# Gate and up products of two row blocks in one pass over the weight tiles, and two attention numerators moved to a later pass

## The chip, the cores and the metric

The kernel runs on one NeuronCore of a Trainium2 chip. The metric is the device time of one execution in microseconds, lower is better. Times of one kernel scatter by some tenths of a microsecond from run to run.

The profile's names: PE is TensorE's row of matmuls, PEld its row of weight loads, DVE is VectorE, ACT is ScalarE, POOL is GpSimd. SBUF is the on-chip memory that holds inputs and weights; PSUM is where matmuls write, used here as eight banks of 512 columns. L361 is line 361 of the kernel.

## The reference

A gated mix of two branches over the same x of 2048 x 640 (bf16). What matters here:

```python
a = attention(x)                                   # linear attention, 32 heads of 20
b = (gelu(x @ w_gate) * (x @ w_up)) @ w_down       # 640 -> 1728 -> 640
g = sigmoid((x * gate_w).sum(-1, keepdims=True))
return g * a + (1 - g) * b
```

The attention ends, for each tile of 128 rows, in a numerator and a denominator (`num = phi_q @ kv`, `den = phi_q @ z`) and their quotient.

## The kernel before

x lies transposed in SBUF (`xT`), in four blocks of 512 columns (rows of x). The 1728 inner features are cut in 13 chunks of 128 and one of 64. For a full chunk, gate is five matmuls (contraction 640 = 5 x 128) into one PSUM bank, and up is five into another. For the last one ("chunk 13"), gate and up share one set of five matmuls and one bank. ScalarE then makes gelu of the gate bank, and VectorE multiplies it by the up bank:

```python
def gateup(self, b, c, banks):
    ...
    slot = self.gn % 3
    self.gn += 1
    if c < 13:
        for w, wk, bk in ((self.wg_sb, "wg", banks[0]), (self.wu_sb, "wu", banks[1])):
            for kt in range(self.KD):                # KD = 5
                self.mm(bk, 0, 512, w[:, kt, c * P:(c + 1) * P], xs(kt), kt == 0, kt == self.KD - 1, ...)
        sc.op("act", lambda e: e.activation(self.gl[:, slot, :], self.bank(banks[0]), AF.Gelu_apprx_tanh), ...)
        sc.op("dve", lambda e: e.tensor_tensor(hT, self.bank(banks[1]), self.gl[:, slot, :], ALU.mult), ...)
    else:
        ...   # chunk 13: five matmuls, one gelu of 64 rows, two half products of 64 rows
```

`self.mm` issues a matmul that always brings its own weight load. The chunks run in the order 0, 1, 13, 2, ..., 12. I call their position in that order the *place*, so chunk 13 stands at place 2. Full chunks alternate between the bank pairs (0,1) and (6,7): a pair is wanted again two places later.

The numerator of a tile is twenty small matmuls into banks 2 to 5, then a chain of eleven VectorE instructions (reciprocals, products with 32 columns, two products and a sum with 640 columns), and at its end a transposing DMA into `goT`:

```python
def num(self, t):
    for i in range(self.KD):
        for s in (0, 1):
            for r in (0, 1):
                ... matmul of 64 rows x 88 columns into bank NUMB + 2 * r + s ...
    ... eleven VectorE instructions, one after the other ...
```

```python
def first_nums(idx):
    if idx in (4, 8):                        # after places 4 and 8
        self.num(idx // 4 - 1)
...
gateups(0, state)
gateups(1, first_nums)
gateups(2, none)
gateups(3, none)
for b in range(self.NB):
    downs(b, ...)                            # w_down and wo, with the other 14 numerators
```

The timelines show VectorE's instructions in the order in which the program issues them.

The softmax here doesn't subtract the row's maximum and nothing guards it: scores larger than these inputs give would overflow.

Of the kernel before, what the change touches and what calls it, by code (L numbers as in the profile page):

```python
# [3 lines left out]
P = 128  # L4
BF16 = mybir.dt.bfloat16
F32 = mybir.dt.float32
AF = mybir.ActivationFunctionType
ALU = mybir.AluOpType
# [99 lines left out]
class _Kernel:  # L108
# [528 lines left out]
            return self.xT[:, c // 3, (c % 3) * self.BT:(c % 3 + 1) * self.BT]  # L637
        return (self.hT0, self.hT1, self.hT2)[b][:, c, :]

    def gateup(self, b, c, banks):  # L640
        sc = self.sc
        xs = lambda kt: self.xT[:, kt, b * self.BT:(b + 1) * self.BT]
        xr = [("xT", t) for t in range(4 * b, 4 * b + 4)]
        old = (self.oldw, self.oldk, [], [("xT", t) for t in range(12)])[b]
        hT, hk = self.hT(b, c), b
        slot = self.gn % 3
        self.gn += 1
        if c < 13:
            i = 0 if c < 7 else 1
            for w, wk, bk in ((self.wg_sb, "wg", banks[0]), (self.wu_sb, "wu", banks[1])):  # L650
                for kt in range(self.KD):
                    self.mm(bk, 0, 512, w[:, kt, c * P:(c + 1) * P], xs(kt), kt == 0, kt == self.KD - 1, xr + [(wk, i)])
            sc.op("act", lambda e: e.activation(self.gl[:, slot, :], self.bank(banks[0]), AF.Gelu_apprx_tanh),  # L653
                  reads=[("ps", banks[0])], writes=[("gl", slot)], guard=self.oldw)
            sc.op("dve", lambda e: e.tensor_tensor(hT, self.bank(banks[1]), self.gl[:, slot, :], ALU.mult),  # L655
                  reads=[("ps", banks[1]), ("gl", slot)], writes=[("hT", hk, c)], guard=old)
        else:
            bk = banks[0]
            for kt in range(self.KD):
                self.mm(bk, 0, 512, self.wgu_sb[:, kt, :], xs(kt), kt == 0, kt == self.KD - 1, xr + ["wgu0", "wgu1"])  # L660
            sc.op("act", lambda e: e.activation(self.gl[64:128, slot, :], self.ps[0:64, bk * 512:bk * 512 + 512],
                                                AF.Gelu_apprx_tanh),
                  reads=[("ps", bk)], writes=[("gl", slot)], guard=self.oldw)
            for r in (0, 1):
                odd = lambda v: v.rearrange("p (u r q) -> p u r q", r=2, q=P)[:, :, r, :]
                sc.op("dve", lambda e: e.tensor_tensor(
                    odd(hT[64 * r:64 * r + 64, :]), odd(self.ps[64:128, bk * 512:bk * 512 + 512]),
                    odd(self.gl[64:128, slot, :]), ALU.mult),
                    reads=[("ps", bk), ("gl", slot)], writes=[("hT", hk, c, r)], guard=old)

    def num(self, t):
        sc = self.sc
# [113 lines left out]
    def ffn(self):  # L786
        self.gn = 0
        self.pn = 0
        pairs = [(0, 1), (6, 7)]

        def gateups(b, after):
            for idx, c in enumerate([0, 1, 13] + list(range(2, 13))):
                self.gateup(b, c, pairs[self.pn % 2])
                self.pn += 1
                after(idx)

        def downs(b, side):
            p = [pairs[(self.pn + k) % 2] for k in (0, 1)]
            n = 0
            for t in (4 * b, 4 * b + 2):  # L800
                final = t + 2 == self.NT
                for _ in self.down_pair(t, p + [(2, 3)] if final else p, (256, 256, 128) if final else (320, 320)):
                    n += 1
                    if n in side:
                        self.num(side[n])

        def state(idx):
            if idx < 3:
                self.gram(13 + idx)
            if idx == 2:  # L810
                self.columns = False
                self.kv_evac()
                self.gates()
                self.kv_ones()
            if 6 <= idx < 11:
                self.kv_mask(idx - 6)

        def first_nums(idx):
            if idx in (4, 8):
                self.num(idx // 4 - 1)  # L820

        def none(idx):
            pass
        at = (1, 31, 61, 91)
        gateups(0, state)
        gateups(1, first_nums)
        gateups(2, none)
        gateups(3, none)
        for b in range(self.NB):
            downs(b, {at[k]: 4 * b + 2 + k for k in range(4 if b < 3 else 2)})  # L830

# [43 lines left out]
```

## Time and profile before

| | before |
|---|---|
| time, median | 286.4 us (286.36 to 286.82) |
| span of the profiled run | 285.0 us |
| matmuls (PE), busy | 281.1 us (99%) |
| weight loads (PEld), busy | 186.1 us (65%) |
| VectorE busy / ScalarE busy | 174.4 / 105.2 us |

The first part of the page: each engine, its busy time, the share of the span and the number of instructions.

```profile
PE 281.1 (99%) x3045; PEld 186.1 (65%) x3060; DVE 174.4 (61%) x352; ACT 105.2 (37%) x200; POOL 5.3 (2%) x36
```

The chain that ended last, by engine and by line, is all TensorE:

```profile
PE 99%; issue 0%; ACT 0%
PE ps L361 62%; PE ps L737 28%; PE ps L681 2%; PE ps L373 2%; PE ps L468 2%; PE ps L341 1%; PE ps L557 1%; PE ps L298 0%; ACT outsb L750 0%; PE ps L564 0%; PE ps L323 0%
```

PE busy at 99% alone does not say that nothing is to be had: matmuls are pipelined, and their records (379 ns each) overlap. What counts is the distance from one matmul to the next. It can be read from VectorE's timeline in the pass of block 1, where nothing but PE paces it. The columns are start, duration, what ran, and in brackets the idle time before it and what ended it.

```profile
103.85 0.69 DVE L655 TENSOR_TENSOR hT<-ps,gl 128x512 bf16<-128x512 f32 x1 [0.72 <-PE ps L361]
106.01 0.69 DVE L655 TENSOR_TENSOR hT<-ps,gl 128x512 bf16<-128x512 f32 x1 [1.47 <-PE ps L361]
108.17 0.69 DVE L655 TENSOR_TENSOR hT<-ps,gl 128x512 bf16<-128x512 f32 x1 [1.47 <-PE ps L361]
110.32 0.69 DVE L655 TENSOR_TENSOR hT<-ps,gl 128x512 bf16<-128x512 f32 x1 [1.47 <-PE ps L361]
112.48 0.69 DVE L655 TENSOR_TENSOR hT<-ps,gl 128x512 bf16<-128x512 f32 x1 [1.47 <-PE ps L361]
```

One product per chunk; four chunks of ten matmuls take 112.48 - 103.85 = 8.63 us, so 215.8 ns a matmul of 512 columns. The Trainium skill (TensorE: Matmul & The Clock Gate, "Wait — 56ns, not 53.3ns?") gives N/2.4 + about 2.5 ns for back-to-back matmuls, 215.7 ns for N = 512. The trace agrees, and it does so with a weight load in front of every matmul. The groups of these loads, from the list that keeps shapes apart:

```profile
L361 PEld LDWEIGHTS ps<-xT,wu_sb 128*128 128x128 bf16 x250 | 24.5, 98 | 29.5
L361 PEld LDWEIGHTS ps<-xT,wg_sb 128*128 128x128 bf16 x250 | 24.2, 98 | 29.0 <-ACT gl L653 0.2
```

A load takes 98 ns (the second number after the bar). It runs beside the matmul in front of it, and in this stage the load row is idle more than half the time.

The first numerator, in block 1 of the kernel before, first PE's timeline and then VectorE's:

```profile
116.81 1.03 PE L361 MATMUL ps<-xT,wu_sb 128*128 128x512 bf16 x4
117.77 0.57 PE L681 MATMUL ps<-KV,Eq 64*128 64x88 bf16 x20
118.27 1.25 PE L361 MATMUL ps<-xT,wg_sb 128*128 128x512 bf16 x5
...
122.60 1.24 PE L361 MATMUL ps<-xT,wg_sb 128*128 128x512 bf16 x5
123.89 1.03 PE L361 MATMUL ps<-xT,wu_sb 128*128 128x512 bf16 x4
```

```profile
117.88 0.69 DVE L655 TENSOR_TENSOR hT<-ps,gl 128x512 bf16<-128x512 f32 x1 [1.47 <-PE ps L361]
118.59 0.36 DVE L697 RECIPROCAL RH<-ps 128x32 f32<-128x32 f32 x1
...
122.31 0.49 DVE L710 TENSOR_TENSOR Og<-O,O 128x640 bf16<-128x640 bf16 x1
122.72 1.28 DVE L655 TENSOR_TENSOR hT<-ps,gl 128x512 bf16<-128x512 f32 x2
```

The chain holds VectorE from 118.59 to 122.72, 4.13 us. The product of the chunk after the numerator (place 5) waits behind it and ends at 122.72 + 0.69 = 123.41. PE wants that chunk's up bank again for place 7, right after the gate matmuls that began at 122.60, that is at 122.60 + 5 x 0.2158 = 123.68. (The up group at 123.89 shows four matmuls: the record of its first, at 123.67, is missing.) So the numerator fits with 0.27 us to spare.

### The profile page before, as it was taken

To read this page: it belongs to the slowest core of one execution; us is meant where nothing else is said; L and a number is where in the kernel's file an instruction comes from. 1 tells how busy PE (TensorE), PEld (TensorE's weight loads), DVE (VectorE), ACT (ScalarE), POOL (GpSimd) and SP (SyncE) were. 2 spreads that over 40 slices of the span, in tenths; PEclk is the share of its full clock that TensorE was granted. 3 is DMA by queue.
4 is the path that set the end of the run, shared out by engine and by line. 5 is a ranking of instruction groups with operands and counts; after the bars stand their busy time and mean duration, and the time that the engine had idled before them with its cause. 6 is when DMAs were issued, how large, how long until landed. Compare 5 with 4: busy or idle time off the path is not lost.

```text
span 285.0 us, 7066 instructions
## 1 busy us (share of the span) xinstructions
PE 281.1 (99%) x3045; PEld 186.1 (65%) x3060; DVE 174.4 (61%) x352; ACT 105.2 (37%) x200; POOL 5.3 (2%) x36
## 2 busy tenths in 40 slices
PE   8999999999999999999999999999999999999996
PEld 4665799999984444444444444445777777777786
DVE  1459999999976652667242334225883883883801
ACT  4367898667754223222322223221112112112021
POOL 7000000000000000000000000000000000000000
DMA  8999993000002000011000000000233223322421
GB/s 228 225 199 313 361 349 111 2 0 2 2 0 48 0 0 2 2 23 25 0 0 0 2 0 0 0 2 0 26 82 58 50 62 59 70 52 68 71 72 48
DMA packets 36937, 18.67 MB, mean 66 GB/s; under 512 B 28970, under 2 KB 36394, under 8 KB 36906
## 3 DMA queue, kind: packets, MB, share of 16 engines
q1 hardware_dynamic: 36240, 18.19, 26.3%
q8 instruction: 24, 0.39, 0.6%
q10 hardware_dynamic: 666, 0.03, 0.2%
q14 instruction: 7, 0.06, 0.1%
HBM read 9.04 MB, written 2.62 MB: 41 GB/s over the span
## 4 chain that ended last, share of the span: by engine, by line
PE 99%; issue 0%; ACT 0%
PE ps L361 62%; PE ps L737 28%; PE ps L681 2%; PE ps L373 2%; PE ps L468 2%; PE ps L341 1%; PE ps L557 1%; PE ps L298 0%; ACT outsb L750 0%; PE ps L564 0%; PE ps L323 0%
## 5 line engine op out<-in xcount | busy, mean ns | idle before, releaser
L361 PE MATMUL ps<-xT,wg_sb 128*128 128x512 bf16 (+1 forms) x265 | 63.8, 379 | 0.4 <-issue 0.2
L361 PE MATMUL ps<-xT,wu_sb 128*128 128x512 bf16 (+1 forms) x263 | 63.3, 379 | 0.4
L653 ACT ACTIVATE gl<-ps 128x512 bf16<-128x512 f32 x52 | 30.9, 596 | 72.9 <-PE ps L361 70.7
L655 DVE TENSOR_TENSOR hT<-ps,gl 128x512 bf16<-128x512 f32 x39 | 26.6, 689 | 38.8 <-PE ps L361 38.7
L737 PE MATMUL ps<-wd_sb,hT 64*128 64x320 bf16 x648 | 48.5, 296 | 0.0
L361 PEld LDWEIGHTS ps<-xT,wu_sb 128*128 128x128 bf16 (+1 forms) x270 | 26.6, 99 | 29.5
L361 PEld LDWEIGHTS ps<-xT,wg_sb 128*128 128x128 bf16 (+1 forms) x270 | 26.2, 99 | 29.0 <-ACT gl L653 0.2
L361 PE MATMUL ps<-w,xT 128*64 128x512 bf16 (+6 forms) x398 | 41.5, 325 | 0.1
L750 ACT ACTIVATE outsb<-ps,Gm 128x320 bf16<-128x320 f32 (+2 forms) x31 | 14.5, 515 | 72.4 <-PE ps L737 72.4
L737 PEld LDWEIGHTS ps<-wd_sb,hT 64*128 64x128 bf16 x648 | 31.1, 94 | 12.2 <-issue 0.4
L361 PEld LDWEIGHTS ps<-w,xT 128*64 128x64 bf16 (+1 forms) x400 | 35.9, 107 | 4.5
L737 PE MATMUL ps<-wo_sb,goT 64*128 64x320 bf16 (+2 forms) x340 | 26.5, 288 | 0.0
L361 PE MATMUL ps<-xT,wq 128*64 128x512 bf16 (+1 forms) x184 | 26.0, 380 | 0.1
L438 DVE TENSOR_REDUCE Dk<-Ek 128x64 f32<-128x1280 bf16 x16 | 23.7, 1478 | 3.7 <-ACT gcol L426 3.7
L452 DVE TENSOR_TENSOR Ek<-Ek,Dk 128x640 bf16<-128x640 bf16 x32 | 25.0, 821 | 0.6
L708 DVE TENSOR_TENSOR O<-ps,RH 128x640 bf16<-128x640 f32 x32 | 24.7, 815 | 0.0
L423 ACT ACTIVATE Ek<-ps 128x640 bf16<-128x640 f32 x32 | 20.7, 703 | 4.2 <-PE ps L361 4.2
L537 ACT ACTIVATE Eq<-ps 128x512 bf16<-128x512 f32 x40 | 21.6, 607 | 0.6 <-PE ps L361 0.4
L655 DVE TENSOR_TENSOR xT<-ps,gl 128x512 bf16<-128x512 f32 x13 | 9.0, 690 | 18.2 <-PE ps L361 18.2
L737 PEld LDWEIGHTS ps<-wo_sb,goT 64*128 64x128 bf16 x340 | 16.0, 94 | 5.3
L361 PEld LDWEIGHTS ps<-xT,wq 128*64 128x64 bf16 (+1 forms) x185 | 15.4, 108 | 2.9
L737 PE MATMUL ps<-wd_sb,xT 64*128 64x320 bf16 (+2 forms) x270 | 16.0, 269 | 0.0
(71 smaller groups left out, 173.8 us busy)
## 6 DMA issues: line engine op xcount, KB each, us to landing
out_dram<-outsb SPq DMA_DIRECT2D x7, 320.0 KB, 2.3
wd_sb<-in_B_w_down_dram SPq DMA_DIRECT2D x1, 2080.0 KB, 12.9
wg_sb<-in_B_w_gate_dram SPq DMA_DIRECT2D x1, 1120.0 KB, 7.4
wu_sb<-in_B_w_up_dram SPq DMA_DIRECT2D x1, 1120.0 KB, 9.8
wg_sb<-in_B_w_gate_dram SPq DMA_DIRECT2D x1, 960.0 KB, 9.1
wu_sb<-in_B_w_up_dram SPq DMA_DIRECT2D x1, 960.0 KB, 9.3
w<-in_A_wqkv_dram SPq DMA_DIRECT2D x5, 160.0 KB, 3.6
wo_sb<-in_A_wo_dram SPq DMA_DIRECT2D x1, 800.0 KB, 8.5
```

The lines of the kernel that those rows point to most:

```text
L361: self.sc.op("pe", lambda e: e.matmul(self.ps[a:z, bank * 512 + c0:bank * 512 + c0 + n], lhs[:, a:z], rhs, start=first, stop=fin), reads=r ...
L373: sc.op("pe", lambda e, c0=c0, n=n, bk=bk, col=col: e.matmul(self.bank(bk)[:, col:col + n], self.xT[:, kt, t * P:(t + 1) * P], self.w3[:, ...
L423: self.sc.op("act", lambda e, s=s, scale=scale: e.activation(self.Ek[:, se, s, :], self.ps[:, o:o + self.D], AF.Exp, scale=scale), reads=[ ...
L438: sc.op("dve", lambda e: e.tensor_reduce(self.Dk[:, se, 0, :].rearrange("p (s h) -> p s h", h=H), self.Ek[:, se, :, :].rearrange("p s (h d ...
L452: sc.op("dve", lambda e, v=v, r=r: e.tensor_tensor(v, v, r, ALU.mult), reads=[("Rk", se)], writes=[("Ek", se, s)])
L468: sc.op("pe", lambda e: e.matmul(self.ps[a:a + 64, b * 512 + c:b * 512 + c + 2 * nf], va[:, lo:lo + 64], self.Ek[:, se, :, f0:f0 + nf], st ...
L537: sc.op("act", lambda e, s=s, scale=scale: e.activation(self.Eq[:, s, i, b * self.BT:(b + 1) * self.BT], self.bank(bank), AF.Exp, scale=sc ...
L653: sc.op("act", lambda e: e.activation(self.gl[:, slot, :], self.bank(banks[0]), AF.Gelu_apprx_tanh), reads=[("ps", banks[0])], writes=[("g ...
L655: sc.op("dve", lambda e: e.tensor_tensor(hT, self.bank(banks[1]), self.gl[:, slot, :], ALU.mult), reads=[("ps", banks[1]), ("gl", slot)], ...
L708: dve(lambda e, o=o, f=f, s=s: e.tensor_tensor(o, V[s][:, :, :, 0:DH], f, ALU.mult), rb + [key(6 + s)], [("O", s, sl)], guard=old)
L737: sc.op("pe", lambda e: e.matmul(self.bank(bk, w), lhs, rhs, start=opens and x == 0, stop=end and not opens, skip_group_check=True), reads ...
L750: sc.op("act", lambda e: e.activation(dst, self.bank(bk, w), AF.Copy, scale=g), reads=rd, writes=wr)
```

## The change

The intent: take blocks 1 and 2 in one pass, so that each tile of w_gate and w_up is loaded once and used by two matmuls, one for each block. The second of a pair is issued without a weight load. The joint pass needs four banks for a chunk and four for the next, all eight, so no numerator fits into it; the first two numerators move to block 3's pass.

```diff
+    def mm_again(self, bank, n, lhs, rhs, first, fin, reads):
+        ...   # InstMatmult(..., ldweights=False): uses the weights that are in the array
-    def gateup(self, b, c, banks):
+    def gateup(self, bs, c, gate, up):
...
+        def mms(w, keys, banks):
+            for kt in range(self.KD):
+                for k, b in enumerate(bs):
+                    a = (512, w(kt), xs(b, kt), kt == 0, kt == self.KD - 1, xr(b) + keys)
+                    if k:
+                        self.mm_again(banks[k], *a)
+                    else:
+                        self.mm(banks[k], 0, *a)
...           # gelu and product as before, once for each block of bs
         def first_nums(idx):
-            if idx in (4, 8):
-                self.num(idx // 4 - 1)
+            if idx in (2, 6):
+                self.num((idx - 2) // 4)
...
-        gateups(0, state)
-        gateups(1, first_nums)
-        gateups(2, none)
-        gateups(3, none)
+        gateups((0,), state)
+        gateups((1, 2), none)
+        gateups((3,), first_nums)
```

More of the change, by code (lines that the diff above doesn't have):

```diff
@@ L638, in hT, with emit @@
         return (self.hT0, self.hT1, self.hT2)[b][:, c, :]
-    def gateup(self, b, c, banks):
-        sc = self.sc
-        xs = lambda kt: self.xT[:, kt, b * self.BT:(b + 1) * self.BT]
-        xr = [("xT", t) for t in range(4 * b, 4 * b + 4)]
-        old = (self.oldw, self.oldk, [], [("xT", t) for t in range(12)])[b]
-        hT, hk = self.hT(b, c), b
-        slot = self.gn % 3
-        self.gn += 1
+    def mm_again(self, bank, n, lhs, rhs, first, fin, reads):
+        nc = self.nc
+        def emit(e):
+            return nc.tensor.add_instruction(mybir.InstMatmult(
+                name=nc.get_next_instruction_name(), engine=mybir.EngineType.PE, start_tensor_calc=first,
+                stop_tensor_calc=fin, tile_size=(P, P), tile_position=(0, 0), ldweights=False,
+                ins=[e.lower_ap(rhs), e.lower_ap(lhs)], outs=[e.lower_ap(self.bank(bank, n))]))
+        self.sc.op("pe", emit, reads=reads, writes=[("ps", bank)], signal=fin)
@@ new lines, in gateup @@
+    def gateup(self, bs, c, gate, up):
+        sc = self.sc
+        xs = lambda b, kt: self.xT[:, kt, b * self.BT:(b + 1) * self.BT]
+        xr = lambda b: [("xT", t) for t in range(4 * b, 4 * b + 4)]
+        slots = [(self.gn + k) % 3 for k in range(len(bs))]
+        self.gn += len(bs)
+        def mms(w, keys, banks):
[6 more added lines that the diff above has]
+                        self.mm(banks[k], 0, *a)
@@ L648, in gateup @@
         if c < 13:
             i = 0 if c < 7 else 1
-            for w, wk, bk in ((self.wg_sb, "wg", banks[0]), (self.wu_sb, "wu", banks[1])):
-                for kt in range(self.KD):
-                    self.mm(bk, 0, 512, w[:, kt, c * P:(c + 1) * P], xs(kt), kt == 0, kt == self.KD - 1, xr + [(wk, i)])
-            sc.op("act", lambda e: e.activation(self.gl[:, slot, :], self.bank(banks[0]), AF.Gelu_apprx_tanh),
-                  reads=[("ps", banks[0])], writes=[("gl", slot)], guard=self.oldw)
@@ L655, in gateup @@
-            sc.op("dve", lambda e: e.tensor_tensor(hT, self.bank(banks[1]), self.gl[:, slot, :], ALU.mult),
-                  reads=[("ps", banks[1]), ("gl", slot)], writes=[("hT", hk, c)], guard=old)
-        else:
-            bk = banks[0]
-            for kt in range(self.KD):
-                self.mm(bk, 0, 512, self.wgu_sb[:, kt, :], xs(kt), kt == 0, kt == self.KD - 1, xr + ["wgu0", "wgu1"])
-            sc.op("act", lambda e: e.activation(self.gl[64:128, slot, :], self.ps[0:64, bk * 512:bk * 512 + 512],
+            mms(lambda kt: self.wg_sb[:, kt, c * P:(c + 1) * P], [("wg", i)], gate)
@@ new lines, in gateup @@
+            mms(lambda kt: self.wu_sb[:, kt, c * P:(c + 1) * P], [("wu", i)], up)
+        else:
+            mms(lambda kt: self.wgu_sb[:, kt, :], ["wgu0", "wgu1"], gate)
+        for k, b in enumerate(bs):
+            old = (self.oldw, self.oldk, [], [("xT", t) for t in range(12)])[b]
+            hT, slot, bg, bu = self.hT(b, c), slots[k], gate[k], up[k]
+            if c < 13:
+                sc.op("act", lambda e: e.activation(self.gl[:, slot, :], self.bank(bg), AF.Gelu_apprx_tanh),
+                      reads=[("ps", bg)], writes=[("gl", slot)], guard=self.oldw)
+                sc.op("dve", lambda e: e.tensor_tensor(hT, self.bank(bu), self.gl[:, slot, :], ALU.mult),
+                      reads=[("ps", bu), ("gl", slot)], writes=[("hT", b, c)], guard=old)
+                continue
+            sc.op("act", lambda e: e.activation(self.gl[64:128, slot, :], self.ps[0:64, bg * 512:bg * 512 + 512],
@@ L662, in gateup @@
                                                 AF.Gelu_apprx_tanh),
-                  reads=[("ps", bk)], writes=[("gl", slot)], guard=self.oldw)
+                  reads=[("ps", bg)], writes=[("gl", slot)], guard=self.oldw)
             for r in (0, 1):
@@ L666, in gateup @@
                 sc.op("dve", lambda e: e.tensor_tensor(
-                    odd(hT[64 * r:64 * r + 64, :]), odd(self.ps[64:128, bk * 512:bk * 512 + 512]),
+                    odd(hT[64 * r:64 * r + 64, :]), odd(self.ps[64:128, bg * 512:bg * 512 + 512]),
                     odd(self.gl[64:128, slot, :]), ALU.mult),
-                    reads=[("ps", bk), ("gl", slot)], writes=[("hT", hk, c, r)], guard=old)
+                    reads=[("ps", bg), ("gl", slot)], writes=[("hT", b, c, r)], guard=old)
     def num(self, t):
@@ L789, in ffn, with gateups @@
         pairs = [(0, 1), (6, 7)]
-        def gateups(b, after):
+        def gateups(bs, after):
             for idx, c in enumerate([0, 1, 13] + list(range(2, 13))):
-                self.gateup(b, c, pairs[self.pn % 2])
+                if len(bs) == 1:
+                    g, u = pairs[self.pn % 2]
+                    self.gateup(bs, c, [g], [u])
+                else:
+                    k = 4 * (self.pn % 2)
+                    self.gateup(bs, c, [k, k + 1], [k + 2, k + 3])
                 self.pn += 1
```

## The prediction

> **What bounds the kernel now.** One stream on TensorE. The page's first part has PE busy 281.1 of 285.0 us (99%), and the chain of waits is 99% PE. In the gate/up stage (about 84 to 197 us) the timeline shows one VectorE product every 2.16 us, that is ten 512-column matmuls: four chunks in 8.63 us, 215.8 ns per matmul. The Trainium skill (TensorE: Matmul & The Clock Gate, "Wait — 56ns, not 53.3ns?") gives N/2.4 + about 2.5 ns = 215.7 ns for back-to-back matmuls with 512 columns; this trace agrees within 0.1 ns. So the stage already runs at the streaming rate, with a weight load before every matmul.
>
> **What the change removes.** 27 x 5 = 135 weight loads of blocks 1 and 2. Each takes 98 ns on the weight-load row (PEld, which overlaps PE), starts with the matmul before it and is over long before that matmul's 216 ns are. It is hidden. Matmuls (270), columns, evictions and DMA are unchanged. Expected: nothing. If the ~2.5 ns above 512/2.4 were the cost of switching weights, 135 x 2.5 ns = 0.3 us would be saved (an estimate from the page's figure; chance one in five).
>
> **What it moves.** The numerators of tiles 0 and 1 go to block 3, after places 2 and 6 instead of 4 and 8. Their PE cost stays: before, 0.59 us each (last gate/up matmul finished streaming at 117.68, next starts at 118.27). But place 2 is the half-width chunk 13. Its VectorE work (two products, together 0.89 us, which wait for the ACTIVATE) ends 1.78 us after PE left it, against 0.9 us for an ordinary chunk, so the numerator's VectorE chain of 4.13 us starts 0.9 us later. The product of the next chunk (place 3) stands behind that chain on VectorE, and its up bank is wanted again at place 5. With T the end of chunk 13 on PE: product done at T + 1.80 + 4.13 + 0.69 = T + 6.62; PE wants the bank at T + 0.59 + 25 x 0.2158 = T + 5.99. Before, the same sum gave 0.3 us of slack; now PE should stall about 0.65 us, once. The second numerator (place 6, ordinary chunk) keeps its slack.
>
> **On the critical path.** Gains 0 to 0.3 us, loss about 0.65 us; 286.4 + 0.65 - 0.05.
>
> **Predicted time: 287.0 us, 8 in 10 between 286.2 and 287.6.** Faster by over 2%: 0.02; within 2%: 0.95; slower by over 2%: 0.03.
>
> **What would show it in the profile.**
> - Weight loads 135 fewer (3060 to 2925), PEld busy about 13 us less (135 x 98 ns), PE busy almost unchanged.
> - In the joint pass matmuls still 215 to 216 ns apart, the one without a load like the one with; blocks 1 and 2 together about 58.3 us.
> - One PE gap of 0.5 to 0.7 us in block 3, in front of the up matmuls of place 5, ended by VectorE's product; no such gap at the second numerator.
>
> **What would make it wrong.**
> - Matmuls without a load run faster than 215.8 ns: the pass would be up to 0.3 us shorter.
> - The load for the next pair is not brought forward past a matmul that has none: then about 0.1 us is exposed per pair, up to 13 us (over 4% slower).
> - VectorE's chain in block 3 starts earlier, no stall: 286.3.

## The result, and the profile after

The changed kernel takes 287.1 us (median of 4, 286.84 to 287.24), the kernel before 286.4 us. The ratio is 1.002 with a 95% interval of 1.0002 to 1.0037. Here and below, a ratio compares the runs of one kernel with the other's of the same rounds, so it is not quite the ratio of the medians.

The first part of the page after:

```profile
PE 282.0 (99%) x3060; PEld 172.6 (60%) x2925; DVE 173.2 (61%) x352; ACT 103.7 (36%) x200; POOL 5.3 (2%) x36
```

135 loads fewer (3060 to 2925) and 13.5 us less time on the load row, and nothing of it shows in the time. From the list of groups by shape, the matmuls that have no load, and then the loads:

```profile
L645 PE MATMUL ps<-xT,wg_sb 128*128 128x512 bf16 x65 | 24.6, 379 | 0.0
L645 PE MATMUL ps<-xT,wu_sb 128*128 128x512 bf16 x65 | 24.6, 379 | 0.0
```

```profile
L361 PEld LDWEIGHTS ps<-xT,wu_sb 128*128 128x128 bf16 x185 | 18.0, 98 | 36.6 <-issue 21.4 <-DVE xT L679 1.0 <-DVE hT L687 0.3
L361 PEld LDWEIGHTS ps<-xT,wg_sb 128*128 128x128 bf16 x185 | 17.8, 98 | 35.4 <-issue 21.7 <-ACT gl L677 0.2
```

The load row now has 43 us of "issue" idle in these two groups, time in which it waits for nothing. Idle time of an engine that does not bound the kernel buys nothing. (The page's summary of the chain is a worse guide here than before: from the end of the stall described below it follows VectorE and ScalarE back to 172.13 us, and only then PE again.)

PE's timeline in the joint pass: L361 is the matmul with a load, L645 the one without.

```profile
113.01 0.38 PE L361 MATMUL ps<-xT,wg_sb 128*128 128x512 bf16 x1
113.22 0.38 PE L645 MATMUL ps<-xT,wg_sb 128*128 128x512 bf16 x1
113.44 0.38 PE L361 MATMUL ps<-xT,wg_sb 128*128 128x512 bf16 x1
113.66 0.38 PE L645 MATMUL ps<-xT,wg_sb 128*128 128x512 bf16 x1
113.87 0.38 PE L361 MATMUL ps<-xT,wg_sb 128*128 128x512 bf16 x1
```

They follow each other at the same 215 to 216 ns. From the first matmul of the pass (start 108.261) to the first of block 3 (166.536) are 58.275 us for 270 matmuls: 215.8 ns, the old figure.

Block 3's pass around the first numerator, after; PE first, then VectorE:

```profile
170.85 1.24 PE L361 MATMUL ps<-xT,wgu_sb 128*128 128x512 bf16 x5
172.03 0.56 PE L702 MATMUL ps<-KV,Eq 64*128 64x88 bf16 x20
172.53 1.25 PE L361 MATMUL ps<-xT,wg_sb 128*128 128x512 bf16 x5
...
176.85 1.24 PE L361 MATMUL ps<-xT,wg_sb 128*128 128x512 bf16 x5
178.61 1.25 PE L361 MATMUL ps<-xT,wu_sb 128*128 128x512 bf16 x5 [0.51 <-DVE xT L679]
```

```profile
172.82 0.89 DVE L687 TENSOR_TENSOR xT<-ps,gl 64x256 bf16<-64x256 f32 x2 [1.08 <-ACT gl L682]
173.74 0.36 DVE L718 RECIPROCAL RH<-ps 128x32 f32<-128x32 f32 x1
...
177.46 0.49 DVE L731 TENSOR_TENSOR Og<-O,O 128x640 bf16<-128x640 bf16 x1
177.87 1.28 DVE L679 TENSOR_TENSOR xT<-ps,gl 128x512 bf16<-128x512 f32 x2
```

Here is the whole loss. PE wanted the up bank at 176.85 + 5 x 0.2158 = 177.93; the product of place 3 that frees it ended at 177.87 + 0.69 = 178.56, and PE went on at 178.61. The bracket says 0.51 us, because it counts idle time from the end of the last matmul's 379 ns record; by the starts in the trace, 177.716 and 178.606, the distance is 890 ns in place of 216, a loss of 0.67 us. It is the only wait of that kind in the list of who waited for whom; before has none:

```profile
PE ps L361 <- DVE xT L679: 0.5, 1, 0.5
```

The chip's noise has to be set apart. I cut each profiled run at two points of the trace, the start of the first matmul that reads w_gate and of the first that reads w_down:

| profiled run | until the gate/up stage | gate/up stage | down stage | span |
|---|---|---|---|---|
| before | 77.72 | 118.965 | 88.319 | 285.0 |
| after | 78.01 | 119.650 | 88.318 | 286.0 |

The gate/up stage is longer by 0.685 us. The stage before it has the same code in both and differs by 0.30 us; over all profiled runs it took between 77.7 and 78.4 us, whatever the kernel. The down stage does not move by more than a nanosecond. So 0.69 us is what the change costs, and the rest of a difference of one pair of runs is scatter of the first stage.

### The profile page after: what moved, and what is told of

Its sections match the earlier page's. It is cut to its first block, busy times and chain, and to the rows that moved or that the text cites. A ratio compares the mean times of both kernels' runs of the same rounds, so it can differ in the third digit from the quotient of the medians.

```text
span 286.0 us, 6946 instructions
## 1 busy us (share of the span) xinstructions
PE 282.0 (99%) x3060; PEld 172.6 (60%) x2925; DVE 173.2 (61%) x352; ACT 103.7 (36%) x200; POOL 5.3 (2%) x36
## 4 chain that ended last, share of the span: by engine, by line
PE 92%; DMA 3%; DVE 2%; SPq 2%; issue 1%; ACT 0%; DVEq 0%
PE ps L361 49%; PE ps L758 28%; PE ps L645 10%; DMA wkT<-in_A_wqkv_dram 3%; PE ps L702 2%; PE ps L468 2%; PE ps L341 1%; SPq L236 1%; SPq L224 1%; DVE O L729 1%; SPq L216 0%; DVE xT L679 0%; ACT gl L682 0%; DVE xT L687 0%; DVE RH L718 0%
## 5 line engine op out<-in xcount | busy, mean ns | idle before, releaser
L361 PE MATMUL ps<-xT,wu_sb 128*128 128x512 bf16 (+1 forms) x205 | 57.2, 379 | 0.5 <-DVE xT L679 0.5
L361 PE MATMUL ps<-xT,wg_sb 128*128 128x512 bf16 (+1 forms) x205 | 57.2, 379 | 0.0
L677 ACT ACTIVATE gl<-ps 128x512 bf16<-128x512 f32 x52 | 29.5, 595 | 75.0 <-PE ps L361 72.8
L679 DVE TENSOR_TENSOR hT<-ps,gl 128x512 bf16<-128x512 f32 x39 | 25.6, 687 | 47.8 <-PE ps L361 47.7
L361 PEld LDWEIGHTS ps<-xT,wu_sb 128*128 128x128 bf16 (+1 forms) x205 | 20.2, 99 | 36.6 <-issue 21.4
L361 PE MATMUL ps<-w,xT 128*64 128x512 bf16 (+6 forms) x400 | 41.9, 325 | 0.0
L361 PEld LDWEIGHTS ps<-xT,wg_sb 128*128 128x128 bf16 (+1 forms) x205 | 19.8, 99 | 35.4 <-issue 21.7
L361 PEld LDWEIGHTS ps<-w,xT 128*64 128x64 bf16 (+1 forms) x400 | 35.9, 107 | 4.5
L361 PE MATMUL ps<-xT,wq 128*64 128x512 bf16 (+1 forms) x185 | 26.2, 380 | 0.0
L645 PE MATMUL ps<-xT,wg_sb 128*128 128x512 bf16 x65 | 24.6, 379 | 0.0
L645 PE MATMUL ps<-xT,wu_sb 128*128 128x512 bf16 x65 | 24.6, 379 | 0.0
L361 PEld LDWEIGHTS ps<-xT,wq 128*64 128x64 bf16 (+1 forms) x185 | 15.4, 108 | 2.9
```

The lines of the kernel that those rows point to most:

```text
L361: self.sc.op("pe", lambda e: e.matmul(self.ps[a:z, bank * 512 + c0:bank * 512 + c0 + n], lhs[:, a:z], rhs, start=first, stop=fin), reads=r ...
L645: return nc.tensor.add_instruction(mybir.InstMatmult(name=nc.get_next_instruction_name(), engine=mybir.EngineType.PE, start_tensor_calc=first,
L679: sc.op("dve", lambda e: e.tensor_tensor(hT, self.bank(bu), self.gl[:, slot, :], ALU.mult), reads=[("ps", bu), ("gl", slot)], writes=[("hT ...
```

## The experiments

The theory (A): the shared loads are worth nothing, since they were hidden; the loss is one stall of PE, and it comes from the numerator's place behind the half-width chunk. The rivals: (B) the joint pass itself costs about 0.6 us, by its waits or its matmuls without a load; (C) the pass saves some tenths and the stall costs more than the net; (D) it matters where the numerator stands on PE, not on VectorE.

### joint_places_4_8: the joint pass without the stall

```diff
-            if idx in (2, 6):
-                self.num((idx - 2) // 4)
+            if idx in (4, 8):
+                self.num(idx // 4 - 1)
```

> The changed kernel with the two numerators after places 4 and 8 of block 3, where an ordinary full-width chunk comes before them. Theory A (the joint pass is worth nothing, the whole loss is one PE stall behind the numerator of place 2): 286.4 us, no matmul start in block 3 later than its neighbours allow except at the two numerators (about 810 ns from the last gate/up matmul before to the next after). Rival B (the joint pass itself costs about 0.6 us, by its extra waits or its matmuls without a load): stays at 287.0 us. Rival C (the joint pass saves some tenths and the stall is larger than the loss): 286.1 us or less.

Measured: 286.58 us against 286.5 us of before (11 runs), ratio 1.0003 (0.999 to 1.0015). In its trace the gate/up stage took 118.965 us, to the nanosecond what it takes before. Around the first numerator, PE reaches the up matmuls of place 7, which need the bank that is freed behind the chain, without a gap (182.00 is 1.08 us, five matmuls, after 180.92):

```profile
176.10 0.57 PE L702 MATMUL ps<-KV,Eq 64*128 64x88 bf16 x20
...
180.92 1.24 PE L361 MATMUL ps<-xT,wg_sb 128*128 128x512 bf16 x5
182.00 1.24 PE L361 MATMUL ps<-xT,wu_sb 128*128 128x512 bf16 x5
```

That is A. B and C are out: the joint pass by itself neither costs nor saves anything.

### move_only: the numerators moved, every load kept

```diff
 # the kernel before
         def first_nums(idx):
-            if idx in (4, 8):
-                self.num(idx // 4 - 1)
+            if idx in (2, 6):
+                self.num((idx - 2) // 4)
...
-        gateups(1, first_nums)
+        gateups(1, none)
         gateups(2, none)
-        gateups(3, none)
+        gateups(3, first_nums)
```

> The kernel before, a weight load for every matmul, with only the two numerators moved to places 2 and 6 of block 3. Theory A: 287.0 us, with the same 0.67 us stall before the up matmuls of place 5 as the changed kernel. Rival B: 286.4 us. Rival C: more than 287.1 us.

Measured: 287.17 us, ratio 1.0021 (1.0009 to 1.0033), the time of the full change. The gate/up stage took 119.656 us, 0.691 more than before. Its timeline has the stall at the same spot, with a load in front of each matmul (the row of the load row first, then PE's; the record of the first of the five up matmuls is missing, so the bracket on PE is 0.2 us too long):

```profile
178.50 0.76 PEld L361 LDWEIGHTS ps<-xT,wu_sb 128*128 128x128 bf16 x5 [1.01 <-DVE xT L655]
178.73 1.03 PE L361 MATMUL ps<-xT,wu_sb 128*128 128x512 bf16 x4 [0.74 <-DVE xT L655]
```

So the move alone makes the whole difference, and the two halves of the change add up: 0 and 0.69 us.

### joint_places_1_6: the first numerator one place earlier

If the reckoning on VectorE's order is right, it should also foretell a stall of another size at another spot.

```diff
-            if idx in (2, 6):
-                self.num((idx - 2) // 4)
+            if idx in (1, 6):
+                self.num(idx // 6)
```

> The changed kernel with the first numerator after place 1 in place of place 2. Theory A, same reckoning: the VectorE chain now stands in front of the two products of the half-width chunk (place 2), whose bank PE wants already at place 4: bank free at T + 0.91 + 4.13 + 0.89 = T + 5.93, wanted at T + 0.59 + 1.08 + 2.16 = T + 3.83 (T the end of place 1 on PE), a stall of 2.1 us before the gate matmuls of place 4 and none at place 5: 288.5 us. Rival B, under which the numerators' places do not matter: 287.0 us.

Measured: 288.98 us (288.5 expected), ratio 1.0097 (1.0073 to 1.0122). One of the six runs, unprofiled, took 291.06 us at a granted clock of 0.994; it is in the ratio, and the other five took 288.72 to 289.13 us at 1.0. In the profiled one the gate/up stage took 121.306 us, 2.34 more than before. The stall stands before the gate matmuls of place 4, ended by chunk 13's products (L687), and nowhere else:

```profile
176.00 0.88 DVE L687 TENSOR_TENSOR xT<-ps,gl 64x256 bf16<-64x256 f32 x2
...
177.03 1.24 PE L361 MATMUL ps<-xT,wg_sb 128*128 128x512 bf16 x5 [2.18 <-DVE xT L687]
```

Spot and releaser are as expected, the size is 0.24 us above the 2.1. The trace shows where that lies. From the chain's first instruction to the product behind it were 4.25 us here (171.75 to 176.00), 0.12 more than the 4.13 I used. And PE began 0.15 us after the product's end (176.88 to 177.03), not 0.05 us as at the stall of the changed kernel: this bank had to be released by two engines, and PE spent a separate semaphore instruction (51 ns, at 176.92) on one of the two waits before it could begin the load.

### joint_chain_after_product: same place on PE, other order on VectorE

```diff
-            if idx in (2, 6):
-                self.num((idx - 2) // 4)
+            if idx == 2:
+                self.num_matmuls(0)          # the twenty matmuls only
+            if idx == 3:
+                self.num_chain(0)            # VectorE's chain, now behind the product of place 3
+            if idx == 6:
+                self.num(1)
```

> The changed kernel with the first numerator's matmuls still after place 2, but its VectorE chain issued after the product of place 3, so that this product no longer stands behind the chain. Theory A: the stall before place 5 is gone; the product of place 4 now stands behind the chain instead, done at T + 3.66 + 4.13 + 0.69 = T + 8.48 against T + 0.59 + 3 x 2.158 + 1.08 = T + 8.15 wanted, a stall of 0.3 to 0.4 us before the up matmuls of place 6: about 286.75 us. Rival D (the stall comes from where the numerator's matmuls stand on PE, not from VectorE's order): the stall stays before place 5, 287.0 us.

Measured: 286.83 us, ratio 1.0009 (0.9997 to 1.0021), which by the times alone is not told apart from before. The trace tells: the gate/up stage took 119.252 us, 0.29 more than before. The gap before the up matmuls of place 5 is gone, and one before those of place 6 has come:

```profile
179.46 1.28 DVE L679 TENSOR_TENSOR xT<-ps,gl 128x512 bf16<-128x512 f32 x2
...
180.20 0.76 PEld L361 LDWEIGHTS ps<-xT,wu_sb 128*128 128x128 bf16 x5 [0.60 <-DVE xT L679]
180.20 1.25 PE L361 MATMUL ps<-xT,wu_sb 128*128 128x512 bf16 x5
```

By the starts it is 490 - 216 = 274 ns, slightly under the expected 0.3 to 0.4 us. PE's order had not been touched; D is out.

### narrow128 and narrow64: when does a weight load cost anything?

The changed kernel's idea would pay where a load is longer than what hides it. The load's record is 98 ns, so I expected it to show with matmuls of 128 columns (56 ns) at the latest. In the kernel before, the 135 matmuls of block 3 are cut in pieces, with a load for each piece (`load`, SHARE false below) or only for the first (`share`, SHARE true). The result is correct in all of them.

```diff
+    def mm_wide(self, b, bk, lhs, rhs, first, fin, reads):
+        ...                                   # blocks 0 to 2 as before
+        for c in range(0, 512, n):            # n = 128, 64 or 32
+            end = fin and c + n == 512
+            if c and SHARE:
+                self.mm_again(bk, c, n, lhs, rhs[:, c:c + n], False, end, reads)
+            else:
+                self.sc.op("pe", ...matmul with a load into columns c to c + n of the bank...)
```

> The kernel before with the 135 matmuls of block 3 each cut into four of 128 columns, a weight load for each of the 540. Asks when a weight load stops being hidden: it takes 98 ns on the load row and the matmul it hides behind now streams for about 56 ns. If a load must end before the next matmul starts: about 100 ns apart, block 3 longer by 540 x 100 - 135 x 216 ns = about 25 us. If loads overlap one another: 56 to 80 ns apart, 1 to 14 us longer.

> The same 540 matmuls, one load for each four. If sharing hides it all: 128/2.4 + 2.5 = 56 ns apart, block 3 longer by 540 x 56 - 135 x 216 ns = about 1.1 us, 287.5 us. If the 2.5 ns above the streaming time belonged to the load, the three matmuls without one would be 53.3 ns apart and the total near 286.4 us.

> The 135 matmuls of block 3 cut into eight of 64 columns, a load for each of the 1080. [...] If the load sets the rhythm, the distance is the same as with 128 columns and loads (the load's own pace), and block 3 grows by 1080 times that minus 29 us; if it is hidden still, about 29 ns apart and 2.5 us longer.

> The same 1080 matmuls, one load for each eight. If sharing hides the load: 64/2.4 + 2.5 = 29 ns apart, block 3 longer by 1080 x 29 - 135 x 216 ns = about 2.5 us, 289 us. Against the run with loads this shows what sharing a load is worth where the load is not hidden.

| columns | with a load each | one load shared | gate/up stage, load / share |
|---|---|---|---|
| 512 (before) | 215.8 ns apart | (after) 215.8 ns | 118.965 / - |
| 128 | 55.8 ns | 55.8 ns | 119.977 / 119.978 us |
| 64 | 29.3 ns | 29.2 ns | 121.458 / 121.328 us |

Times, medians of two runs each against 286.6 us of before: 287.73 and 287.57 us with 128 columns, 289.01 and 289.13 us with 64. (The 0.13 us by which the stage with loads is longer at 64 columns is one gap, of 164 ns from start to start, before the matmul at 193.15.) My 100 ns, and the 56 to 80 ns in case of overlap, gave way to the lowest figure: a load of 98 ns is hidden behind 29 ns of matmul. Its record is a latency. One window of eight microseconds in the run with 64 columns and loads and one in the run that shares them show it:

```profile
182.00:190.00 8.00, 8.00 (x281) 8.00 (x278) 2.08 (x3) 2.29 (x4) 0.00 (x0) 1.00 0.02 4
```

```profile
182.00:190.00 8.00, 8.00 (x280) 3.33 (x34) 2.08 (x3) 2.39 (x4) 0.00 (x0) 1.00 0.01 2
```

The columns are the window, its length, then busy time and count of PE, PEld, DVE, ACT and POOL. In the first, 278 loads of 98 ns stand in 8.00 us, so some three at a time are under way; the load row is 100% busy and the matmuls come at the same rate as in the second, where it is at 42%. A load row that is full says nothing of a limit. One rival has to be looked at: with 64 columns, seven of eight loads bring weights that are in the array already, and might cost nothing for that reason. But the first of the eight brings new ones, and in the trace it starts 27 to 29 ns before its matmul, about as the others do, its record is 98 ns long, and the distance between matmuls is 29.3 ns there too. The expected 53.3 ns for matmuls without a load did not come either, so the 2.5 ns above pure streaming does not belong to the load.

### narrow32: the last place to look

> The 135 matmuls of block 3 cut into sixteen of 32 columns, a load for each of the 2160. With 64 columns a matmul with a load came every 29.3 ns, so a load takes the array for at most 29.3 ns whatever its 98 ns on the load row say. [...] If the load's own pace shows here, the distance stays between 16 and 29 ns, longer than in the run with sharing; if matmul and load overlap wholly even here, the two runs agree.

> The same 2160 matmuls, one load for each sixteen. By streaming plus 2.5 ns they would be 16 ns apart; if issuing sets a floor of about 25 ns (the Trainium skill, TensorE: Matmul & The Clock Gate, states one), about 25 ns with and without loads, and sharing a load is worth nothing at any width: block 3 then takes 2160 x 25 = 54 us against 29 us, about 311 us in all.

Measured: 311.3 us with a shared load, as expected, with a matmul every 25.0 ns; the Trainium skill (the same page, "Wait — 56ns, not 53.3ns?") states that start-to-start never falls below about 25 ns, and this run agrees. With loads it was 319.76 us (318.41 and 321.12). Neither of the two expected cases came: the times differ, and yet the load does not pace the matmuls here either. The mean distance, 29.4 ns, would look like the load's own pace, but the median is again 25.0 ns, and so are the tenth and ninetieth percentiles. The 9.4 us more of gate/up stage lie in 15 gaps of 0.3 to 0.8 us from start to start (9.75 us in all, 9.4 above the regular 25 ns), most of them some 4 us apart:

```profile
180.09 0.28 PE L662 MATMUL ps<-xT,wu_sb 128*128 128x32 bf16 x5
180.27 0.60 ACT L679 ACTIVATE gl<-ps 128x512 bf16<-128x512 f32 x1 [1.41 <-PE ps L662]
180.99 0.59 PEld L662 LDWEIGHTS ps<-xT,wu_sb 128*128 128x128 bf16 x21 [0.74 <-issue]
181.00 0.67 PE L662 MATMUL ps<-xT,wu_sb 128*128 128x32 bf16 x20 [0.64 <-issue]
```

PE waits there for nothing that the profile names. In the trace the transfers of the program's own instructions, 16 KB each, come at that same rhythm, one every 3.5 to 4.2 us over most of the pass against about 6 us in the run that shares its loads, and each of the 15 gaps ends 1.2 to 1.6 us after such a transfer does. The transfers alone don't stop PE: in narrow64_load they come every 3.5 to 4.0 us of the pass, and there is only the one gap of 164 ns. All this fits an engine that ran out of instructions, since loads double their number; I did not test it apart, so it stays a likely cause and not a shown one.

No experiment points to a version that beats both kernels: joint_places_4_8 removes the stall, and what remains is the time of the kernel before.

## Why the prediction was right

It said 287.0 us, within 286.2 to 287.6; 287.1 was measured. That alone proves little: the range also holds 286.4, the time of a change without any effect. What bears the prediction out is the mechanism, point by point:

- *The stage already runs at the streaming rate.* Right: 215.8 ns a matmul before, 215.8 ns in the joint pass.
- *The removed loads were hidden, gain nothing.* Right: 135 fewer, 13.5 us less on their row (13 predicted), and joint_places_4_8 has a gate/up stage of 118.965 us like before. The narrow runs go further than I had thought: my reason was that 98 ns fit under 216 ns, but 98 ns also "fit" under 29 ns.
- *One chance in five for 0.3 us, if the 2.5 ns were the cost of switching weights.* They are not: 55.8 ns with 128 columns with and without loads.
- *The numerator behind chunk 13 stalls PE by about 0.65 us, before the up matmuls of place 5.* Right: 0.67 us, there, ended by VectorE's product. With T = 171.93 the product ended at T + 6.63 (6.62 predicted) and the bank was wanted at T + 6.00 (5.99).
- *The second numerator keeps its slack.* Right: its last matmul before and first after stand 810 ns apart, as at both numerators of the kernel before, and no other gap follows.
- *Loss and no gain sum to the result.* move_only, with 0.691 us more gate/up stage, and joint_places_4_8, with 0.000, show it apart.
- *PE busy almost unchanged.* 281.1 to 282.0 us. PE's busy share cannot show any of this; both are 99%.

What gave the right answer was to carry VectorE's order through the moved code instruction by instruction. The move looked free, since the numerator had the same banks and the same cost on PE. But its old place had 0.27 us of slack, and the half-width chunk in front of the new one delays VectorE by 0.9 us: its gate and up come from the same five matmuls, so the gelu and both products (172.13 to 173.71) are still to be done when PE leaves it at 171.93, while behind an ordinary chunk only the product is.

## What to carry to other kernels

Before sharing a weight load, measure the distance between matmuls: if it is the streaming time of the moving columns, the load is hidden, and the length of its record or the share of a busy load row does not say otherwise; here it was hidden at every width at which the matmul itself set the pace. When a long chain on an in-order engine is moved, reckon which result queues up behind it and when the critical engine wants that result's buffer, at the new place and not at the old. Look also at how much eviction is left when PE leaves the item in front of the chain: here 1.8 us behind the half-width chunk, and 0.9 us behind an ordinary one.

## What the Trainium skill lacked or had wrong

- TensorE: Matmul & The Clock Gate, "Back-to-back issue gap": it gives about 131 ns a matmul for N = 512 and about 81 ns for N = 128 in a stream of load and matmul pairs, and calls N/2.4 + 2.5 ns the figure of an isolated matmul. Here such streams ran at 215.8 and 55.8 ns, the "isolated" figures, with a load for every matmul.
- The same page, Part 3, "The mechanism": its list says that a load overlaps a matmul in flight only when their row groups differ, though the paragraph above it also allows a load into a background buffer; the two do not agree. Here full-height loads began some 2 ns after the start of a full-height matmul and ran beside it, in every chunk.
- The same page, "LDWEIGHTS (loading the stationary operand)": columns / 1.2, 107 ns for 128, is near the record's 98 ns, but that section doesn't say that this is a latency, and no measured spacing of bf16 loads stands beside it. Loads followed one another every 29.3 ns with 64-column matmuls, and mostly every 25.0 ns with 32-column ones.
- Perfetto Trace Analysis, "Identifying the Most-Contended Engine": the busy share of weight loads is named, together with MFU (the share of peak matmul work), as a measure of headroom. Here it was 65% before, 60% after and 71% in narrow64_load, and filled its row in that run's block 3, with no effect on the matmuls' rate.
- No page that I found says what it costs when PE waits for two engines for one bank: here, in one stall of each kind, about 0.1 us more from release to matmul (0.15 against 0.05 us), with a separate 51 ns semaphore instruction. (Perfetto Trace Analysis, "Identifying Dependency Chains", mentions such an instruction, without a time.)
